# Sharing three pairs of PSUM banks between attention scores and weighting, with a new task order, in a fused attention and gated feed-forward kernel

## The chip, the cores and the metric

The kernel runs on one core of a Trainium2 chip. The metric is the device time of one execution in microseconds (us), the median of three runs. The core has a matrix engine (PE, with the weight loads shown apart as PEld), a vector engine (DVE), an activation engine (ACT), GpSimd (POOL) and a sync engine (SP); the last two issue the transfers here. Matmuls write to PSUM, which the program cuts into eight banks of 512 fp32 columns, numbered 0 to 7.

## The reference, cut to what matters

Attention over 4 batches, 8 heads, 768 positions and head size 64. Heads 0, 2 and 6 are causal over all keys; the other five see a window of 64 keys and 4 sink keys. The heads are then put side by side to a 3072 x 512 matrix `x`, and a gated feed-forward block with a gated residual follows.

```python
stream_keep = causal & (is_sink | in_win)
mask = np.where(retr[0, :, 0, 0, None, None], full_mask, stream_mask)
scores = np.where(mask[None, :, :, :], scores, -1000000000.0)
a = np.exp(scores - np.max(scores, axis=-1, keepdims=True))
a = a / (np.sum(a, axis=-1, keepdims=True) + 1e-09)
attn_out = np.matmul(a, v)
...
g = x @ w_gate                    # 3072 x 512 times 512 x 1536
val = x @ w_val
ffn_out = gelu(g) * val @ w_out   # 1536 x 512
res_gate = 1.0 / (1.0 + np.exp(-(x @ w_res)))
return (x + res_gate * ffn_out).astype(np.float32)
```

## The kernel before

The program is not written as a fixed sequence. It builds a graph of 1,727 tasks (a task is one instruction, or a few on the same engine), and a list scheduler, which runs while the program is built, puts the tasks of every engine in an order. The engines then run these orders as they stand, with semaphores between them. The 3,072 tokens are worked on in six chunks of 512, numbered c = 0 to 5. For each chunk there are score matmuls (`sc`), exponentials on ACT, masks on DVE, weighting with the values (`win`, `av`, `avk`), normalization on DVE, a transpose to features (`xT`), gate and value matmuls (`g`, `v`), gelu on ACT, the product on DVE (`h`), the residual gate (`res`) and the second feed-forward matmul (`ff`). The attention of one chunk is laid between the `res` and `ff` matmuls of the chunk before it.

Three things decide the order. First, the scheduler gives out PSUM banks. A kind of buffer has a cap (how many may be held at once) and a list of the places it may take, tried from left to right:

```python
P_ps = Psum(psum, {
    "av1": (2, one(0, 1)), "av2": (1, [(0, 1)]), "av1": (3, one(0, 1, 6)),
    "sc": (2, [(2, 3), (4, 5)]), "scr": (3, one(5, 4, 3, 2)), "scr0": (3, one(5, 4, 3, 2)),
    "gv": (4, one(6, 7, 5, 4, 3, 2)), "gv0": (4, one(6, 7, 5, 4)), "gvh": (4, one(7, 6, 4, 5)), "out": (2, one(6, 7)), "warm": (1, one(7, 5)),
})
```

(The key "av1" is written twice; the later one holds.) A score unit takes a pair of banks ("sc"), which the exponentials free. One weighting of a pair of heads takes a pair too ("av2"), from its first matmul until the last of its three DVE instructions, the reciprocal and two normalizations, has read it. Chunk 0 is done in halves and its weighting takes single banks ("av1"). Gate and value matmuls use "gv", and `res` and `ff` use "out". Score units of chunks 1 to 5 go in twos; the first of two takes both places before it starts:

```python
sc = ph(c, "sc")[:-1]
for t, u in zip(sc[0::2], sc[1::2]) if c else ():
    t.deps += u.deps
    u.order.append(t)
    for b in u.bufs[:1]:
        t.bufs.append(b)
        ...
```

Second, the kind of array shape that a PE task uses (`mode`): "row" for the scores (64 x 128), "quarter" for the sink scores (64 x 32), "col" for the windows and the first transposes (128 x 64), and none for all that uses the full array. While the PE is in one of the three special shapes, ready tasks of the same shape come first:

```python
away = e == "pe" and mode is not None and t.mode != mode
p_ = t.prio if t.swap is None or not away else t.swap
key = (int(away), p_, t.seq)          # the smallest key is taken
```

Third, the priorities: a rule gives every task one, and a list `HINTS` ("task:priority") overrides 128 of them.

Until the first gate matmul is ready, the PE is kept busy with matmuls of zeros (line 1178, `warm`), whose results nobody reads; the first gate task ends them.

Of the kernel before, what the change touches and what calls it, by code (L numbers as in the profile page):

```python
# [43 lines left out]


HINTS = (
    "0:-96.05 3:-32.5 13:-14.98 398:-205.14 399:-3161.01 400:-242.48 401:-60.67 406:194.11 428:585.68 "
    "430:523.84 442:461.16 444:1172.07 587:-105.78 592:-108.69 613:396.07 617:407.42 620:-11.7 640:556.2 "
    "642:106.88 643:194.09 646:-2979.21 649:-102.44 659:511.02 686:-2.88 687:77.5 695:496.52 696:499.45 "
    "698:-3129.77 703:60.14 704:-184.95 705:-133.38 707:183.02 708:380.49 711:7.46 712:149.85 713:-50.64 "  # L50
    "715:-14.97 722:1121.95 725:480.98 726:449.69 731:-39.24 732:60.67 733:-318.24 737:-43.72 738:419.39 "
    "739:143.85 743:67.93 744:-230.75 746:-318.2 749:428.99 755:137.07 756:5.66 757:60.69 761:-9.34 "
    "762:495.92 764:2489.99 778:1098.32 789:2479.4 791:2501.2 807:953.41 837:1156.8 842:1419.06 877:2567.99 "
    "879:1563.79 880:2429.98 883:2507.13 898:1013.73 933:1964.55 937:1029.47 939:1471.24 940:2476.14 "
    "955:3421 962:3506.26 963:3575.25 971:3584.03 984:2490.73 989:3565.66 1020:3589.17 1022:2520.47 "
    "1036:2494.69 1066:3486.98 1103:3422.44 1109:3530.5 1114:4315.61 1115:4410.02 1124:-926.78 1134:4596.47 "
    "1141:3465.41 1143:2510.98 1146:2495.35 1152:4653.43 1157:112.2 1170:3039.97 1193:107.93 1248:3488.54 "
    "1265:3479.95 1266:4395.47 1271:4430.01 1272:4484.04 1275:-26.92 1284:5420.01 1289:3472.11 1290:4444.38 "
    "1293:-34.14 1295:3453.61 1302:4490.78 1305:3510.02 1316:3998.02 1318:3550.85 1319:3550.87 1320:4107.35 "
    "1349:3529.55 1351:5429.99 1355:3583.42 1414:5485.04 1451:1066.16 1462:4552.31 1474:4473.03 1475:6343.89 "  # L60
    "1480:4497.31 1530:6505.9 1534:2349.36 1556:5501.98 1602:6498.99 1637:6513.87 1670:7448.62 1687:7406.44 "
    "1689:5504.27 "
)

class Task:
# [396 lines left out]
def build_kernel(nc, q, k, v, w_gate, w_val, w_out, w_res, out):  # L462
# [32 lines left out]
    psum = nc.alloc_psum_tensor("ps", [128, 8 * 512], FP32)  # L495
    one = lambda *bs: [(b,) for b in bs]
    P_ps = Psum(psum, {
        "av1": (2, one(0, 1)), "av2": (1, [(0, 1)]), "av1": (3, one(0, 1, 6)),
        "sc": (2, [(2, 3), (4, 5)]), "scr": (3, one(5, 4, 3, 2)), "scr0": (3, one(5, 4, 3, 2)),
        "gv": (4, one(6, 7, 5, 4, 3, 2)), "gv0": (4, one(6, 7, 5, 4)), "gvh": (4, one(7, 6, 4, 5)), "out": (2, one(6, 7)), "warm": (1, one(7, 5)),  # L500
    })

# [726 lines left out]
def bass_duo_attention_split__then__geglu_gated_residual_kernel(  # L1229
    nc: bass.Bass,  # L1230
    q: bass.AP,
    k: bass.AP,
    v: bass.AP,
    is_retrieval: bass.AP,
    n_sink: bass.AP,
    window: bass.AP,
    moe_w_gate: bass.AP,
    moe_w_val: bass.AP,
    moe_w_out: bass.AP,
    moe_w_res: bass.AP,  # L1240
    out: bass.AP,
):
    assert int(n_sink) == N_SINK and int(window) == WINDOW
    build_kernel(nc, q, k, v, moe_w_gate, moe_w_val, moe_w_out, moe_w_res, out)
# [33 lines left out]
```

The softmax here doesn't subtract the row's maximum and nothing guards it: scores larger than these inputs give would overflow.

## Time and profile before

| | |
|---|---|
| time, median of 3 runs | 270.63 us (270.5 to 271.09) |
| span of the profiled execution | 268.8 us |
| PE busy | 264.2 us (98%), 2391 matmuls |
| DVE busy | 140.1 us (52%) |
| ACT busy | 139.9 us (52%) |
| POOL busy | 87.3 us (32%) |
| PE clock granted | 1.000 of full speed, throughout |

A line of the profile's list of groups gives the source line, the engine, the operation, the tiles written and read, the shapes and the count, then the busy time of the group and the mean of one instruction in ns, then the idle time ahead of them and what ended it. Source lines that matter here: 857 scores, 948 sink scores, 981 windows, 991 weighting of causal heads, 1005 weighting of sinks, 1070 transposes to features, 1098 and 1116 gate and value, 1146 `res`, 1161 `ff`, 1178 the matmuls of zeros, 679 the transposes of queries and keys. Matmuls overlap in the pipeline, so the mean of one (379 ns for 512 columns) is its passage and not its share of the engine; the distance between two starts is the share.

### The profile page before, as it was taken

How to read it: one execution, taken by the hardware profiler on the slowest of the kernel's cores; microseconds unless marked ns; L12 is line 12 of the kernel's file. 1: busy time of each engine (PE TensorE's matmuls, PEld its weight loads, DVE VectorE, ACT ScalarE, POOL GpSimd, SP SyncE). 2: the span in 40 equal slices, each digit the busy share in tenths (PEclk: the TensorE clock that was granted, in tenths of full speed). 3: DMA queues.
4: the chain of work that ended last, by engine and by line, in shares of the span. 5: the costliest groups of instructions: out<-in, count | busy, mean ns of one | idle time of the engine just before them, and what ended most of it. 6: DMA issues, size and time to landing. Idle time of an engine off the chain costs nothing.

```text
span 268.8 us, 5676 instructions
## 1 busy us (share of the span) xinstructions
PE 264.2 (98%) x2391; PEld 138.7 (52%) x2391; DVE 140.1 (52%) x273; ACT 139.9 (52%) x215; POOL 87.3 (32%) x124
## 2 busy tenths in 40 slices
PE   8999999999999999999999999999999999999995
PEld 7677465465444455444455444555444455444444
DVE  2698245485264376445476433486145367534344
ACT  3785358783334877136792243984233788233310
POOL 8999508995808029894000000000000000000000
DMA  6999999999999999999994100022000113200013
GB/s 86 171 205 207 185 180 228 169 168 187 171 129 187 154 160 185 216 189 125 184 148 134 41 0 0 2 41 96 25 0 0 39 41 80 78 2 0 1 39 120
DMA packets 97562, 29.38 MB, mean 109 GB/s; under 512 B 85504, under 2 KB 93952, under 8 KB 97536
## 3 DMA queue, kind: packets, MB, share of 16 engines
q0 software_dynamic: 70320, 14.69, 65.5%
q1 hardware_dynamic: 27216, 14.33, 27.9%
q8 instruction: 19, 0.31, 0.5%
q14 instruction: 7, 0.06, 0.1%
HBM read 29.36 MB, written 6.29 MB: 133 GB/s over the span
## 4 chain that ended last, share of the span: by engine, by line
PE 93%; DMA 3%; POOL 1%; DVE 1%; issue 0%; POOLq 0%; DVEq 0%
PE ps L1116 44%; PE ps L1161 23%; PE ps L1146 8%; PE ps L857 5%; PE ps L991 3%; DMA va<-in_v_dram 3%; PE ps L1098 3%; PE ps L981 2%; PE ps L1005 2%; PE ps L1070 1%; POOL qks L555 1%; PE ps L948 1%; PE ps L679 1%; PE ps L1178 1%; DVE otile L1168 0%; DVE otile L1165 0%
## 5 line engine op out<-in xcount | busy, mean ns | idle before, releaser
L1130 DVE SCALAR_TENSOR_TENSOR hT<-gact,ps 128x512 f16<-128x512 f16 x68 | 45.8, 686 | 67.4 <-ACT gact L1128 36.6
L1128 ACT ACTIVATE gact<-ps 128x512 f16<-128x512 f32 x68 | 40.1, 597 | 74.0 <-PE ps L1116 72.5
L1116 PE MATMUL ps<-xT,wv 128*128 128x512 f16 x272 | 74.3, 379 | 0.0
L1116 PE MATMUL ps<-xT,wg 128*128 128x512 f16 x272 | 74.1, 379 | 0.0
L1161 PE MATMUL ps<-wo,hT 128*128 128x512 f16 (+2 forms) x312 | 70.4, 363 | 0.0
L1116 PEld LDWEIGHTS ps<-xT,wg 128*128 128x128 f16 x272 | 26.3, 98 | 31.5 <-ACT xT L1077 0.6
L1116 PEld LDWEIGHTS ps<-xT,wv 128*128 128x128 f16 x272 | 26.2, 98 | 30.5 <-DVE hT L1130 0.5
L1161 PEld LDWEIGHTS ps<-wo,hT 128*128 128x128 f16 x312 | 27.5, 98 | 27.0 <-issue 0.7
L873 ACT ACTIVATE er<-ps 128x1024 f16<-128x1024 f32 (+4 forms) x40 | 34.2, 891 | 9.5 <-PE ps L857 9.4
L555 POOL DMA_DIRECT2D qks<-in_k_dram x36 | 28.3, 827 | 32.4 <-DMA qkt<-qks 21.9
L555 POOL DMA_DIRECT2D qks<-in_q_dram x36 | 28.8, 840 | 0.8 <-POOLq L1260 0.8
L1165 DVE SCALAR_TENSOR_TENSOR otile<-srs,ps 128x512 f32<-128x512 f32 (+2 forms) x26 | 16.8, 644 | 16.5 <-PE ps L1161 16.4
L1146 PE MATMUL ps<-wr,xT 128*128 128x512 f16 x96 | 24.7, 379 | 0.0
L555 POOL DMA_DIRECT2D va<-in_v_dram x24 | 21.6, 926 | 2.7 <-PE ps L1005 2.7
L1149 ACT ACTIVATE srs<-ps 128x512 f32<-128x512 f32 x24 | 14.3, 597 | 15.6 <-PE ps L1146 15.3
L1048 DVE TENSOR_TENSOR xtok<-ps,rcp 128x512 f32<-128x512 f32 (+1 forms) x28 | 16.9, 609 | 0.6
L1168 DVE TENSOR_TENSOR otile<-otile,xtok 128x512 f32<-128x512 f32 (+2 forms) x26 | 16.8, 647 | 0.7
L857 PE MATMUL ps<-qkt 64*128 64x64 f16 (+4 forms) x391 | 16.9, 213 | 0.0
L857 PEld LDWEIGHTS ps<-qkt 64*128 64x128 f16 x391 | 9.8, 94 | 9.4 <-issue 3.4
L873 ACT ACTIVATE es<-ps 128x1024 f16<-128x1024 f32 (+1 forms) x14 | 12.6, 898 | 2.9 <-PE ps L857 2.6
L1146 PEld LDWEIGHTS ps<-wr,xT 128*128 128x128 f16 x96 | 8.7, 98 | 10.0 <-issue 0.7
L1178 PE MATMUL ps<-blank 128*128 128x128 f16 x116 | 11.4, 249 | 1.1 <-DVE blank L527 1.1
(70 smaller groups left out, 212.5 us busy)
## 6 DMA issues: line engine op xcount, KB each, us to landing
out_dram<-otile SPq DMA_DIRECT2D x23, 256.0 KB, 2.2
va<-in_v_dram POOLq DMA_DIRECT2D x24, 128.0 KB, 17.0
qks<-in_k_dram POOLq DMA_DIRECT2D x32, 64.0 KB, 11.9
qks<-in_q_dram POOLq DMA_DIRECT2D x32, 64.0 KB, 12.4
wg<-in_moe_w_gate_dram POOLq DMA_DIRECT2D x3, 512.0 KB, 10.3
wv<-in_moe_w_val_dram POOLq DMA_DIRECT2D x3, 512.0 KB, 10.6
wo<-in_moe_w_out_dram POOLq DMA_DIRECT2D x4, 384.0 KB, 22.2
vs<-va SPq DMA_DIRECT2D x4, 260.0 KB, 7.4
```

The costliest lines, as they stand in the source:

```text
L555: return G.add(eng, issue, lambda e: e.dma_start(out_ap(), in_ap), deps, prio, bufs=bufs, dma=cost, name=name, grp=grp)
L857: return [e.matmul(at(scr)[:, oo:oo + w], lhsT=side(BB, low, 1)[half, k0:k0 + 128], rhs=side(BB, low, 0)[half, qq:qq + w], start=True, sto ...
L873: return e.activation(out=o, in_=i_, func=AF.Exp, scale=SM_SCALE)
L1048: t2 = G.add("dve", c_dve(2 * n * 64), lambda e: e.tensor_tensor(out=xview(), in0=avv(0, DHEAD), in1=scale(), op=ALU.mult), [t1] + xdeps, ...
L1116: return lambda e: [e.matmul(at(dst)[:, :], lhsT=w[:, ci, f * 128:(f + 1) * 128], rhs=at(xtbuf)[:, ci, :], start=(ci == 0), stop=(ci == NC ...
L1128: ta = G.add("act", c_act(512), (lambda gb=gb, ga=ga: lambda e: e.activation(out=at(ga)[:, :], in_=at(gb)[:, :], func=AF.Gelu))(), [tg], p ...
L1130: th = G.add("dve", c_dve(512), (lambda vb=vb, ga=ga, f=f: lambda e: e.scalar_tensor_tensor(out=at(h)[:, f, :], in0=at(ga)[:, :], scalar=0 ...
L1146: e.matmul(at(rb)[:, :], lhsT=at(xtbuf)[:, ci, s], rhs=wr[:, ci, :], start=(ci == 0), stop=(ci == NCB - 1))
L1149: ta = G.add("act", c_act(512), (lambda rb=rb, sr=sr: lambda e: e.activation(out=at(sr)[:, :], in_=at(rb)[:, :], func=AF.Tanh, scale=0.5)) ...
L1161: e.matmul(at(fb)[:, w], lhsT=at(h)[:, fi, s], rhs=wo[:, fi, w], start=(fi == 0), stop=(fi == NF - 1))
L1165: t1 = G.add("dve", c_dve(n), (lambda fb=fb, sr=sr, ot=ot, w=w: lambda e: e.scalar_tensor_tensor(out=at(ot)[:, w], in0=at(sr)[:, w], scala ...
L1168: t2 = G.add("dve", c_dve(n), (lambda ot=ot, lt=lt, w=w: lambda e: e.tensor_tensor(out=at(ot)[:, w], in0=at(ot)[:, w], in1=at(xbuf)[:, lt, ...
```

## The change

The change shares three pairs of banks, (0, 1), (2, 3) and (4, 5), between scores and weighting. A score unit could use two pairs and can now use three, and up to three units may be held at once instead of two. A weighting could use only (0, 1) and now may use any of the three; two weightings may be held at once instead of one. The caps and places of gate, value and output buffers stay as they were. The list of priorities is replaced: 147 entries for 128, and five of the new ones (marked "~") set the priority that a task has while the PE is in another array shape. No task is added or taken away except matmuls of zeros, whose number follows from the schedule; what can change is the order on each engine, the bank that each buffer gets and so the semaphore waits, and, for the few tasks that may run on either DVE or ACT, the engine. The aim is to let scores and weightings run further ahead and stand closer together.

```diff
 HINTS = (
-    "0:-96.05 3:-32.5 13:-14.98 398:-205.14 399:-3161.01 400:-242.48 401:-60.67 406:194.11 428:585.68 "
...
+    "0:-9.51 2:-52.51 4:-44.21 5:-57.18 6:-1060.04 421:-59.16 428:2066.12 430:2989.94 ~430:3531.29 479:1306.02 "
+    "495:1278.68 524:2561.23 596:-96.42 607:1050.19 614:97.41 633:-66.88 636:205.02 640:382.38 ~640:131.36 "
+    "~644:995.57 648:740.75 657:765.41 662:760 664:759.5 666:349.49 668:100.04 691:4.54 696:2962.41 699:1421.49 "
...
+    "956:2754.07 965:4155.32 971:2503.38 972:65.29 993:2397.82 994:2160.7 1002:1679.16 1004:3164.19 "
+    "~1004:3423.66 1009:3163.69 ~1009:2964.44 1029:7296 1037:3619.4 1060:2504.5 1061:4279.31 1064:1096.39 "
...
     P_ps = Psum(psum, {
-        "av1": (2, one(0, 1)), "av2": (1, [(0, 1)]), "av1": (3, one(0, 1, 6)),
-        "sc": (2, [(2, 3), (4, 5)]), "scr": (3, one(5, 4, 3, 2)), "scr0": (3, one(5, 4, 3, 2)),
+        "av1": (3, one(0, 1, 6)), "av2": (2, [(0, 1), (4, 5), (2, 3)]),
+        "sc": (3, [(2, 3), (4, 5), (0, 1)]), "scr": (3, one(5, 4, 3, 2)), "scr0": (3, one(5, 4, 3, 2)),
         "gv": (4, one(6, 7, 5, 4, 3, 2)), "gv0": (4, one(6, 7, 5, 4)), "gvh": (4, one(7, 6, 4, 5)), "out": (2, one(6, 7)), "warm": (1, one(7, 5)),
     })
```

In the new list, entries 0 to 6 are constants built on DVE and POOL, 421 to 430 the first transposes of queries and keys, 596 to 668 the attention of chunk 0 (`sc`, exponentials, masks, normalization), and nearly all of the rest gate, value, `res` and `ff` matmuls of all chunks, with a few score, window and exponential tasks of chunks 2 to 5 among them. The four old entries that placed the copies of the sink values on POOL (398 to 401) are gone, so these copies fall back to their rule.

## The prediction

> **What bounds the kernel now.** I read the first two parts of the page first, because a change of order can only pay where an engine waits.
>
> ```profile
> span 268.8 us, 5676 instructions
> PE 264.2 (98%) x2391; PEld 138.7 (52%) x2391; DVE 140.1 (52%) x273; ACT 139.9 (52%) x215; POOL 87.3 (32%) x124
> PE   8999999999999999999999999999999999999995
> PE 93%; DMA 3%; POOL 1%; DVE 1%; issue 0%; POOLq 0%; DVEq 0%
> ```
>
> The second line is the busy time of each engine, the third the PE in 40 slices, the fourth the chain that ended last, by engine. All three point to the PE: it is busy in every slice and makes up 93% of the chain. But busy is not yet used well: the page counts a matmul's whole passage. So I went to the chain in order of time, where a run of equal matmuls gives the distance between starts.
>
> ```profile
> 107.93 19.86 PE ps L1116 x92
> 231.29 20.72 PE ps L1116 x96
> ```
>
> The columns are start, duration, what, and how many. 19.86/92 and 20.72/96 are both 216 ns for a matmul of 512 columns. This is the pace of the gate and value matmuls for 20 us on end, with not one gap.
>
> The next view is the PE's timeline between 130 and 147 us, one of the stretches in which the attention of a chunk lies between the `res` and `ff` matmuls of the chunk before.
>
> ```profile
> 130.26 1.90 PE L1161 MATMUL ps<-wo,hT 128*128 128x512 f16 x8
> 132.09 0.56 PE L857 MATMUL ps<-qkt 64*128 64x64 f16 x13
> ...
> 138.51 2.32 PE L1161 MATMUL ps<-wo,hT 128*128 128x512 f16 x10
> 140.67 0.77 PE L991 MATMUL ps<-va,er 128*128 128x65 f16 x20
> ```
>
> The columns are start, duration, engine, line, tiles, the part of the array used, shape and count. From 138.51 to 140.67 there are 2.16 us, 10 matmuls at 216 ns: following work of the same full array (128*128) starts at once. From 130.26 to 132.09 there are 1.83 us where 8 x 216 ns are 1.73: the first score matmul (64*128) starts about 0.1 us late. I took the starts of all PE matmuls from the trace and did this for each neighbouring pair: start to start[...]. After 18.65 us, when the last matmuls of zeros are over, there are 89 changes of array shape, and they cost **94.7 ns each in the mean** (half of them between 93.2 and 95.8 ns), 8.43 us together. All other gaps add up to 0.9 us, and most of that looks like records missing from the trace. So from 18.65 us on, the PE waits for no data and no bank that I can find: it pays for work, and for changing shape.
>
> The rest of the span lies at the two ends. Up to 18.65 us, 116 matmuls of zeros take 10.6 us of the PE (sum of their starts to the next start):
>
> ```profile
> L1178 PE MATMUL ps<-blank 128*128 128x128 f16 x116 | 11.4, 249 | 1.1 <-DVE blank L527 1.1
> ```
>
> These are the wait for the first inputs and for chunk 0's attention, in disguise. At the other end the last matmul starts at 265.67 us and 3.1 us follow for the last gated sum and its transfer.
>
> [...] No wait for a bank shows on the PE before; whether one will after, no run shows yet.
>
> **The change, part by part.**
>
> *Matmul work*: none is added or removed. The gate, value, `res` and `ff` matmuls, the scores and the weightings keep their counts and shapes, so the sum of their 216 ns and smaller pieces stays. This is the bulk: 268.8 us, less 10.6 of zeros, 8.4 of shape changes, 0.9 of gaps, 3.1 at the end and 1.1 ahead of the first matmul leaves about 244.7 us that no order can touch.
>
> *A third score unit and a second weighting*: before, a weighting holds banks (0, 1) until the third DVE instruction has read them. A reciprocal is 0.18 us and each of the two normalizations about 0.6 to 0.7 us (609 ns is the mean of the group at line 1048), so some 1.5 us in which no other weighting can start. And two score units wait for both exponentials, 0.9 us each (891 ns at line 873). The PE fills both waits with `res` and `ff` matmuls, at no loss except two shape changes for each visit. With more banks the scheduler may place scores, sink scores and windows of two head pairs next to each other and save visits. That is the only way in which this part can pay after 18.65 us.
>
> How many changes can go? Counted by stretch, before: 10 from 20 to 43.8 us (chunk 0's second half and a few input transposes), then for the attention of chunks 1 to 5: 17, 16, 13, 16 and 16. Chunk 3 shows what the old scheme reaches at its best, because there a sink score is followed at once by scores and scores three times by windows. If the other four come down to chunk 3's 13, that is 4+3+3+3 = 13 changes, 13 x 94.7 ns = **1.23 us**. With a third unit 11 each could be reached, 13 more changes less, 1.2 us again; I don't count on it, since sticking to a shape is already in the scheduler and most of the new priorities are for full-array matmuls. My choice is 1.2 us.
>
> *The start*: 10.6 us of zeros is the greater reserve, but it hangs on input transfers, POOL's issuing (busy 5.00 of 5 us from 5 to 10 and from 15 to 30 us) and ACT. ACT's timeline before 20 us shows exponentials and copies nearly without a break from 8.6 to 19.7 us; its waits for scores there are 0.67, 0.21 and 0.17 us. A third score place can close some of these, at most 1.05 us. The new priorities also bring two mask constants forward and let four copies on POOL (1.54 us at 12.54 us), which stand ahead of three weight transfers, fall behind some of them. I set the start at -0.2 us, with half a microsecond either way.
>
> *The end*: the tail is 3.1 us of DVE and output transfer that the change does not cut; 0.
>
> *New waits*: gate and value matmuls take banks 6, 7, 5, 4, 3, 2. With (2, 3) or (4, 5) held by late weightings, the first gate matmuls of a chunk can run short where they did not before. I add 0.2 us for that.
>
> The sum: 270.6 - 1.2 - 0.2 + 0.2 = **269.4 us**.
>
> **The rivals.** *The order on paper and the chip part ways*: the priorities are fitted to assumed durations, and the engines run the order as it stands. If an exponential, a normalization or a bank comes later than assumed, the PE stands still at that place[...]. Against it: the order before was made in the same way and shows no such stop in 246 us. For it: every bank of the six is now in use by two or three kinds of buffer, and each reuse is a wait across engines. One stop of 0.4 us at each of five attention stretches is 2 us and eats the gain: 271 us. *ACT takes over*: in the stretches from 85 to 90, 95 to 105 and 135 to 140 us, ACT is busy 4.1 to 4.8 of 5 us. A third score unit then only queues ahead of ACT, no exponential ends earlier, and only the shape changes are left: 269.5 to 270.5 us. *The start sets the gain*: if chunk 0's attention really gets closer together, the first gate matmul, at 19.43 us before, moves up by as much as a microsecond, and since the PE is full from there on, all of it reaches the end: 268.2 us. *All is hidden*: the PE is full already, the visits stay as many, and the time stays at 270.6 us.
>
> **Range and chances.** The centre is 269.4 us. The lower end, 267.8, is both halves of the gain at their best: 25 changes less (2.4 us) and 0.5 us at the start. The upper end, 271.0, is no gain in changes and 0.4 us of new waits. Two per cent are 5.4 us: to be that much faster all shape changes but a few would have to go, or half the zeros at the start, for which I see no ground, so 0.03. To be that much slower the PE would have to stop for over 5 us in some new place, so 0.02. Within 2%: 0.95.
>
> **What would show it.** (1) Runs of gate and value matmuls must still go at 216 ns; if not, all of this reading is wrong. (2) The shape changes after the zeros should fall from 89 to about 76, at the same 95 ns. (3) The zeros' share and the start of the first gate matmul (19.43 us) should move by less than 0.7 us. (4) In the list of waits, the PE should still show no wait of note for DVE or ACT; a new entry of the PE waiting for the normalization or for gelu would be the bank shortage. (5) ACT's idle time waiting for scores at line 873, 9.4 us in 18 waits for the causal heads, should fall without the span falling with it. The prediction fails if shape changes do not fall, if PE gaps appear that belong to no shape change, or if the first gate matmul moves by several microseconds.

## The result: slower by 3.2%, and the profile after

| | before | after |
|---|---|---|
| time, median (lowest to highest) | 270.65 us (same chip, beside the changed kernel) | 279.13 us (278.62 to 280.13, 4 runs) |
| ratio, 95% interval | | 1.0319 [1.0296, 1.0343] |
| span of the profiled execution | 268.8 us | 278.3 us (the slowest of the four) |
| shape changes behind the first gate matmul | 88 | 79 |
| matmuls of zeros, their share of the PE | 116, 10.58 us | 112, 10.25 us |
| start of the first gate matmul | 19.43 us | 19.70 us |
| start of the last PE matmul | 265.67 us | 274.43 us |

The 40 slices and the chain of the changed kernel, from its page:

```profile
span 278.3 us, 5663 instructions
...
PE   8999999999997399999999999999999999999994
...
PEclk9999999999999599999999999999999999999999
...
PE 77%; DMA 16%; POOL 2%; DVE 1%; issue 0%; SPq 0%; DVEq 0%
```

A slice is 7.0 us. In slices 13 and 14 the PE falls to 7 and 3 tenths, and in the 14th its clock to 5 tenths; everywhere else the row is as full as before. The chain that ended last has 16% DMA where it had 3%. So the loss is one hole near 90 us and not many small ones. The stretches around it (columns: window, its length, busy time and count of PE, PEld, DVE, ACT and POOL, clock, DMA engines busy, GB/s):

```profile
85.00:90.00 5.00, 3.75 (x40) 1.60 (x38) 2.46 (x5) 4.13 (x6) 2.81 (x4) 1.00 2.03 166
90.00:95.00 5.00, 0.00 (x0) 0.00 (x0) 0.81 (x2) 0.00 (x0) 0.00 (x0) 0.68 1.59 160
95.00:100.00 5.00, 4.76 (x43) 2.25 (x44) 0.69 (x1) 2.45 (x4) 0.00 (x0) 0.64 1.47 117
```

From 90 to 95 us not one matmul starts. The PE's timeline names what ended the hole, in brackets (idle time, releaser):

```profile
85.99 2.76 PE L1163 MATMUL ps<-wo,hT 128*128 128x512 f16 x12
95.24 0.61 PE L859 MATMUL ps<-qkt 64*128 64x512 f16 x1 [6.49 <-DMA q<-qkt]
...
96.21 3.06 PE L1148 MATMUL ps<-wr,xT 128*128 128x512 f16 x8
99.20 0.61 PE L859 MATMUL ps<-qkt 64*128 64x64 f16 x13
```

(Line numbers are 2 higher than before.) Two things are to be seen. The PE stood for 6.49 us for a transfer, `q<-qkt`, and for no bank. And behind the hole 8 `res` matmuls take 2.99 us from 96.21 to 99.20, where 8 x 216 ns are 1.73: 1.2 us more, at the clock of 0.64 in the window above. With the score matmuls ahead of them, which are slow too, it is 1.6 us.

`q<-qkt` is a copy that SyncE starts: it puts the transposed queries and keys of head 6 for one chunk on the other 64 partitions, where a part of this head's scores is computed. What it waited for stands in the chain in order of time (start, duration, what):

```profile
64.85 21.52 DMA va<-in_v_dram
86.39 0.46 SPq L640
...
87.15 8.05 DMA q<-qkt
...
95.24 1.03 PE ps L859 x16
```

The load of values `va` took 21.52 us from issue to landing. Then SyncE (SPq) issued line 640, and 0.76 us after it the copy `q<-qkt`. Line 640 is `vs<-va`, a copy of these values for the windows, which the PE needs much later. The copy `q<-qkt` does not need the values at all; it only stands behind two copies `vs<-va` in SyncE's order. SyncE's timeline after:

```profile
85.20 1.64 SPq L640 DMA_DIRECT2D vs<-va  x2
87.15 0.66 SPq L732 DMA_DIRECT2D q<-qkt  x1
```

and before:

```profile
80.81 0.67 SPq L730 DMA_DIRECT2D q<-qkt  x1
...
92.76 1.81 SPq L638 DMA_DIRECT2D vs<-va  x3
```

The order of these copies has turned round. The values come no later than before (landed at 86.37 us, before at 87.50). But the copy `q<-qkt` goes out 6.34 us later and lands at 95.20 us instead of 87.58, while the PE is ready for its scores at about 88.7 us. Before, it started them at 88.81 us without a wait:

```profile
87.85 1.03 PE L1161 MATMUL ps<-wo,hT 128*128 128x512 f16 x4
88.81 0.61 PE L857 MATMUL ps<-qkt 64*128 64x64 f16 x13
```

How the order turned can be followed in the scheduler's plan of the two kernels, that is, the times that it gives to all tasks while it makes the order. It assumes that the values for these two copies are there at 72.5 and 74.0 us (on the chip 85.12 and 86.37) and the features for `q<-qkt` at 78.6 us. The plan of the kernel before has them nearly as early (74.5 and 75.4 us), but there transposes of a better priority (1050 against 1051; the smaller goes first) fill SyncE until `q<-qkt` is ready. The new list moves two of these transposes, tasks 479 and 495, back to 1306 and 1279. SyncE then runs out of other work and takes the two copies first. In the plan each of the two entries is needed for this: without either one `q<-qkt` goes first again. They are not enough by themselves: with the same list and the old table of banks the plan has the values at 78 and 79 us, and `q<-qkt` goes first.

### The profile page after: what moved, and what is told of

It is laid out like the page before. It is cut to its first block, busy times and chain, and to the rows that moved or that the text cites. A ratio compares the mean times of both kernels' runs of the same rounds, so it can differ in the third digit from the quotient of the medians.

```text
span 278.3 us, 5663 instructions
## 1 busy us (share of the span) xinstructions
PE 265.9 (96%) x2387; PEld 140.7 (51%) x2387; DVE 140.5 (51%) x272; ACT 138.2 (50%) x216; POOL 87.2 (31%) x124
## 4 chain that ended last, share of the span: by engine, by line
PE 77%; DMA 16%; POOL 2%; DVE 1%; issue 0%; SPq 0%; DVEq 0%
PE ps L1118 35%; PE ps L1163 21%; DMA va<-in_v_dram 8%; PE ps L1148 8%; DMA wv<-in_moe_w_val_dram 5%; PE ps L859 4%; DMA q<-qkt 3%; PE ps L993 3%; PE ps L983 2%; PE ps L1007 1%; PE ps L1100 1%; POOL va L557 1%; PE ps L681 1%; PE ps L1072 1%; PE ps L950 1%; POOL wg L557 1%
## 5 line engine op out<-in xcount | busy, mean ns | idle before, releaser
L1118 PE MATMUL ps<-xT,wv 128*128 128x512 f16 x272 | 72.0, 380 | 0.4 <-DMA wv<-in_moe_w_val_dram 0.4
L1118 PE MATMUL ps<-xT,wg 128*128 128x512 f16 x272 | 71.6, 380 | 0.0
L1163 PE MATMUL ps<-wo,hT 128*128 128x512 f16 (+2 forms) x312 | 69.4, 363 | 0.0
L1148 PE MATMUL ps<-wr,xT 128*128 128x512 f16 x96 | 25.7, 394 | 0.0
L1180 PE MATMUL ps<-blank 128*128 128x128 f16 x112 | 12.1, 262 | 1.1 <-DVE blank L529 1.1
```

The source lines that it names most:

```text
L1118: return lambda e: [e.matmul(at(dst)[:, :], lhsT=w[:, ci, f * 128:(f + 1) * 128], rhs=at(xtbuf)[:, ci, :], start=(ci == 0), stop=(ci == NC ...
L1148: e.matmul(at(rb)[:, :], lhsT=at(xtbuf)[:, ci, s], rhs=wr[:, ci, :], start=(ci == 0), stop=(ci == NCB - 1))
L1163: e.matmul(at(fb)[:, w], lhsT=at(h)[:, fi, s], rhs=wo[:, fi, w], start=(fi == 0), stop=(fi == NF - 1))
```

## The experiments

**Theory A**: the time is lost because `q<-qkt` of chunk 2 stands behind two transfers in SyncE's order that wait for a slow load. The main rivals: the shared banks and the new order of the PE cost it, in many waits; or the new order of transfers on POOL does, by delaying the loads. For the first runs a helper was put behind the scheduler that takes tasks out of one engine's order and puts them ahead of another task; the dependences and the waits are then worked out for that order.

### One copy ahead of two, nothing else

```diff
     span = G.schedule()
+    move("sp", (476,), 491)          # q<-qkt of chunk 2 ahead of the two vs<-va
```

> The changed kernel with one transfer moved in SyncE's order: the copy of half of the features of batch 1 (q<-qkt, 87.15 us in the changed kernel's trace) is issued ahead of the two copies vs<-va of batch 2 (85.20 and 86.39 us) and not behind them. All other engines keep their order. Theory A (the two copies wait for values of batch 2 that land at 86.37 us, and hold up the copy behind them): the copy goes out at about 82.4 us, lands near 89.5 us, the PE waits about 1 us where it waited 6.5 us, the slow clock of the PE after the wait (1.2 us) goes, and the time is 272 to 273 us. Theory B (the banks or the new order of scores make the PE stop there anyway): the wait stays above 5 us and the time above 277 us.

Measured: 271.78 us median of 13 runs (270.59 to 272.67 us, and one of 275.13 us), ratio to the kernel before 1.0035 [1.0018, 1.0051]. The copy was issued at 80.84 us and landed at 87.78. From the PE's timeline:

```profile
87.82 0.39 PE L859 MATMUL ps<-qkt 64*128 64x512 f16 x1 [0.53 <-DMA q<-qkt]
...
88.38 1.90 PE L1148 MATMUL ps<-wr,xT 128*128 128x512 f16 x8
```

The stop has shrunk from 6.49 to 0.53 us, and 8 `res` matmuls are back at 216 ns each (88.38 to 90.21 us, with 0.1 us for the change of shape behind them). One place in one queue, with all banks and all priorities as changed, carries all of the 3.2% but 0.35. The PE runs the same 2,387 matmuls in the same order in both kernels, so their starts can be set against each other. The changed kernel's lag grows by 1.5 us at two value weights, by 6.0 us at the stop and by 1.6 us in the slow matmuls behind it, 9.0 us in all between these two executions. The last two make 7.5 us; the medians differ by 7.35. The value weights are taken up below.

### The mirror: two copies ahead of one in the kernel before

```diff
     span = G.schedule()
+    move("sp", (491, 492), 476)      # the two vs<-va ahead of q<-qkt
```

> The kernel before with the reverse edit: the two copies vs<-va of batch 2 are put ahead of the copy q<-qkt of batch 1 in SyncE's order; banks and priorities as before. Theory A: the values of batch 2 land at 87.50 us in the trace before, so the copy goes out near 89 us instead of 80.81 and lands near 96.5 us; the PE, which needs it at 88.9 us, stops for about 7 us and runs about 3 us at a lower clock after it: 278 to 280 us. Theory B (the banks or the new order of scores are the cause): below 272 us.

Measured: 279.25 us, 4 runs, ratio 1.0321 [1.0306, 1.0337]. From SyncE's and then the PE's timeline:

```profile
83.61 2.63 SPq L638 DMA_DIRECT2D vs<-va  x2
86.54 0.66 SPq L730 DMA_DIRECT2D q<-qkt  x1
```

```profile
94.94 0.61 PE L857 MATMUL ps<-qkt 64*128 64x64 f16 x12 [5.83 <-DMA q<-qkt]
...
95.91 1.89 PE L1161 MATMUL ps<-wo,hT 128*128 128x512 f16 x4
```

With the old banks and the old priorities the same turn of the order makes the whole loss: the same stop, and behind it 4 matmuls in 1.68 us (95.91 to 97.59), 420 ns each. Removal and addition agree, so A is shown as the cause of the loss; how much of the rest the banks and priorities carry is the next question.

### POOL's order as before, beside the first cure

```diff
+    move("sp", (476,), 491)
+    G.prog["pool"][:27] = [... the order of the kernel before ...]
```

> The changed kernel with the copy q<-qkt first, and besides the first 27 POOL instructions (constants, first loads, copies of sink values) in the order of the kernel before. Theory C (the new POOL order lets the first two parts of the value weights land 1.5 and 2.3 us later than before, and the PE waits 0.87 and 0.57 us for them): the two waits go and the time is about 1.4 us under that of the copy first alone, 270.5 to 271.5 us. Rival D (the weights are later [...], whatever the order on POOL): the same time as with the copy first alone, within 0.4 us.

Measured: 271.7 us, 5 runs, ratio 1.0037 [1.0023, 1.0051], the same as without it. POOL's order is not what is left. In the changed kernel's profile the PE had stood idle 0.7 and 0.4 us for value weights (0.87 and 0.57 us when counted between the starts of matmuls); with POOL's order as changed, the first experiment had these weights 1.5 and 2.4 us earlier, so those waits are most likely a spread of the transfers between executions.

### Each half of the change alone

The table of banks alone, with the old priorities:

```diff
-        ... "av2": (1, [(0, 1)]), "av1": (3, one(0, 1, 6)),
-        "sc": (2, [(2, 3), (4, 5)]), ...
+        "av1": (3, one(0, 1, 6)), "av2": (2, [(0, 1), (4, 5), (2, 3)]),
+        "sc": (3, [(2, 3), (4, 5), (0, 1)]), ...
```

> The kernel before with only the table of banks changed: three pairs shared, up to three score units and two weightings; the old priorities. In the order that the scheduler then gives, SyncE issues the copy q<-qkt of batch 1 ahead of the copies vs<-va, so theory A expects no stop of 6 us there. The order has 145 matmuls of zeros instead of 116, so the first gate matmul comes some 1.5 us or more later. Expected 273 to 282 us; if the banks by themselves were a gain, it would lie under 270 us.

The new priorities alone, with the old table (the same two lines, the other way round, in the changed kernel):

> The changed kernel with the old table of banks (two score units, one weighting): only the new priorities are left. In the order that the scheduler then gives, SyncE issues the copy q<-qkt ahead of the copies vs<-va, so theory A expects no stop of 6 us at that place. The priorities were chosen for the other table; the PE changes array shape 129 times instead of 118. Expected: slower than the kernel before by waits at other places, 276 to 288 us; if the priorities by themselves were a gain, under 270 us.

Measured: 278.54 us for the table alone (1.0293 [1.0272, 1.0313]), 290.24 us for the priorities alone (1.0725 [1.07, 1.0751], above the 276 to 288 us expected), 2 runs each. From the list of waits, table alone and then priorities alone (columns: total us, times, longest):

```profile
PE ps L857 <- ACT er L873: 1.9, 2, 1.3
...
PE ps L1070 <- DVE x L1046: 0.9, 1, 0.9
```

```profile
PE ps L983 <- DVE xtok L1050: 3.4, 2, 1.7
...
PE ps L1072 <- DVE x L1048: 2.7, 3, 1.1
...
PE ps L1118 <- DVE xT L1079: 2.2, 4, 0.9
```

In the first, SyncE's order is the good one, and yet the PE stops, for exponentials and normalizations. In the second the windows (line 983) wait for the normalization `xtok` of the weighting before, because there is one place for weightings and the priorities assume two; the transposes (line 1072) and gate and value matmuls (line 1118) then wait for their own late inputs. These two numbers do not add up to the 3.2%: a list of priorities is fitted to one table, and with another it gives another order in all engines. So the halves can't be read as the shares of the change. They show only that the table does not pay without a list of its own. Most of these losses are in the plan already: there the halves take 274.6 and 281.1 us, against 265.5 for the kernel before and 264.7 for the changed one.

### Ahead of the late copy, other work

In the first experiment the PE still waited 0.53 us. Here four `res` matmuls stand ahead of these scores:

```diff
+    move("sp", (476,), 491)
+    move("pe", (971,), 999)          # one res group ahead of the score pair
```

> The changed kernel with the copy q<-qkt first, and on the PE one group of four res matmuls (0.86 us) put ahead of the pair of score units that needs the copy. With the copy first alone the time was 271.78 us in the middle but 270.6 us at its best, and the PE reaches the pair at 87.0 us where the copy lands at 87.8. If that short wait is what is left of the loss (theory A, second half), the time falls by 0.3 to 1 us, to 270.7 to 271.5 us, and scatters less; if the rest comes from elsewhere, it stays at 271.5 to 272.

Measured: 271.46 us, 22 runs, ratio 1.0029 [1.0014, 1.0044]. The wait is gone from the PE's timeline, there is no bracket any more:

```profile
88.54 1.03 PE L1148 MATMUL ps<-wr,xT 128*128 128x512 f16 x4
89.50 0.39 PE L859 MATMUL ps<-qkt 64*128 64x512 f16 x1
```

The median moved by 0.3 us, within the intervals, and the times do not scatter less, as was expected: nine lie from 270.17 to 270.94 us, eight from 272.27 to 272.76 and five between. So the wait of 0.5 us is not what is left. The profiled execution is one of the eight; its first gate matmul starts at 21.09 us, against 19.70 in the profile of the first experiment. ACT's timelines, of the first experiment and then of this one:

```profile
16.86 0.60 ACT L875 ACTIVATE es<-ps 128x512 f16<-128x512 f32 x1 [0.60 <-PE ps L983]
```

```profile
18.26 0.60 ACT L875 ACTIVATE es<-ps 128x512 f16<-128x512 f32 x1 [1.24 <-PE ps L983]
```

Chunk 0's exponentials run 1.4 us later in this execution, where a load of queries had landed at 9.85 us instead of 8.39. The profiled execution with POOL's order as before is of the same kind: first gate matmul at 21.07 us, 272.07 us in all. The likely reading is that the new start hands a late load on to the end, and the old one, whose 27 runs beside these lie between 270.3 and 271.7 us, less so. No run changed the start alone, so this stays open.

### The scheduler told of late loads

In the plan by which the changed order was made, the last of the values that the two copies need is there at 74.0 us. On the chip it landed at 86.37. Here the plan is given later landings, and the list of priorities is searched anew, once with the new table and once with the old:

```diff
+    BB.vtok[i].late = (1.3, 1.3, 10.0, 7.0)[b]             # values of batch b, us
...
+    t.late = 4.0                                          # q<-qkt
+    d.late = (5.0, 5.0, 5.0, 11.0, 8.5, 8.5)[c]            # queries and keys of chunk c
-    HINTS = ...                                           # old list
+    HINTS = ...                                           # list found with these numbers
```

> The new table of banks, with the scheduler told of later landings (values of batch 2 by 8.7 us and of batch 3 by 5.7, queries and keys of chunks 3 to 5 by 6 and 3.5 us, the copies vs<-va by 3 and q<-qkt by 2), as the trace of the kernel before shows them, and the priorities searched anew under these. In its order the copy q<-qkt goes out ahead of the copies vs<-va. Theory A (what was wrong was the assumed landing, not the table): no PE stop near 88 us, 269.5 to 271.5 us. If the shared banks make stops of their own: above 272 us.

> The old table of banks with the same later landings and priorities searched anew in the same way for as long: what the refit does without the shared banks. If the table is worth something, this is slower than the refit with the new table by over 0.5 us; if the table is worth nothing, the two lie within 0.5 us of each other, 269.5 to 271 us.

Measured, on one chip: 272.88 us with the new table (1.0068 [1.0044, 1.0091]), 272.42 us with the old (1.0055 [1.0042, 1.0068]), 6 runs each. The largest wait for data in each:

```profile
PE ps L959 <- DMA q<-qkt: 1.6, 1, 1.6
```

```profile
PE ps L793 <- DMA qks<-in_q_dram: 1.4, 2, 0.8
```

The large hole is gone in both, but both are slower than expected and neither beats the kernel before. The new table's 272.88 us lies where stops by the shared banks were expected (above 272 us); its list of waits names none, its largest wait is for `q<-qkt` again. Under equal treatment the intervals of the two tables overlap: no gain of the shared banks was found. The search was a short one, so this is no proof that there is none.

### One priority taken out

```diff
-    "... 430:2989.94 ~430:3531.29 479:1306.02 "
+    "... 430:2989.94 ~430:3531.29 "
```

> The changed kernel with one of its 147 priorities taken out (that of task 479, a transpose of chunk 3's features that SyncE starts); bank table and all other priorities as changed. The scheduler then has two more of these transposes ahead on SyncE and puts the copy q<-qkt of chunk 2 ahead of the two copies vs<-va by itself, without a hand in the order. From there on the rest of the order differs too. Theory A (a transfer that waits for the values of batch 2 holds up the queue behind it): the copy is issued by 85 us, the PE does not stop for more than 2 us near 88 us, no half clock there, and the time falls to 271 to 275 us; it need not reach the kernel before, because the other priorities were fitted to an order that no longer holds. Rival (the shared banks and the new order of the PE cost the time at many places): the time stays above 277 us.

Measured: 284.65 us, 4 runs, ratio 1.0526 [1.0504, 1.0547]. The expectation failed, and the time lies where the rival had it (above 277 us). `vs<-va` did fall behind `q<-qkt`, and yet the copy was issued at 88.43 us. From the chain in order of time:

```profile
64.69 22.23 DMA qks<-in_q_dram
...
86.94 1.19 SPq L724
...
88.43 6.51 DMA q<-qkt
...
94.98 1.03 PE ps L859 x17
```

The queue was now held by a transpose (line 724) whose queries, of the next chunk, took 22.23 us to land. I had put a name to the blocking transfer and not looked at what else would stand ahead. Of the rest of the 14 us some 4 lie near 117 us: the PE waits 1.93 us for a normalization and 0.61 us for the transposed input, and its clock is 0.84 and 0.82 in the two windows of 5 us from 115 us on, up to 1.7 us more. The plan already has this order as a worse one: 271.1 us without the entry, 264.7 with it.

To see whether this is the same cause with another holder, the copy was put ahead of that one transpose:

```diff
+    move("sp", (476,), 504)          # q<-qkt ahead of the transpose that waits
```

> The kernel of the last run, in which the copy q<-qkt stood behind a transpose that waited for queries of chunk 3 (landed 86.92 us) and was issued at 88.43 us, with this one copy put ahead of that one transpose in SyncE's order; nothing else differs. Theory A (what the PE pays is the place of the copy behind any transfer that waits for a late load): the copy is issued near 81 us, lands by 88.5 us, the stop of 6.4 us near 88.6 us and the half clock behind it (about 1.2 us) are gone, and the time falls from 284.65 by 7 to 8 us, to 276.7 to 277.7 us; the stop of 1.9 us for the normalization near 117 us stays. Rival (a PE that is held up once by late loads is held up a little later by the next one, so that the gain is given back): less than 4 us is gained.

Measured: 276.95 us, 4 runs, ratio 1.0219 [1.0159, 1.0278], 7.7 us less than without it. The copy was issued at 81.76 us and landed at 88.73, the scores started at 88.78 us with no wait on the PE, and the wait for the normalization stayed, as expected. A holds for both holders that were tried: a transfer that waited for a late load held up the ready copy behind it. Of the 6 us that remain against the kernel before, the plan of this order has 5.6 (271.1 against 265.5).

## Why the prediction was wrong, point by point

The prediction was 269.4 us, 267.8 to 271.0; 279.13 us was measured. The differences in the profiled executions, taken from the starts of all matmuls (the changed kernel's is its slowest, so they add up to more than the 8.5 us between the medians):

| term | predicted | measured |
|---|---|---|
| shape changes | -1.2 us (13 fewer) | -0.85 us (9 fewer) |
| start (first gate matmul) | -0.2 us | +0.27 us |
| new waits | +0.2 us | +6.56 us at `q<-qkt`, +1.44 us for value weights |
| PE clock | not considered | +1.57 us |
| other gaps | not considered | -0.2 us |
| last PE start, sum | -1.2 us | +8.76 us (274.43 - 265.67) |
| tail behind it | 0 | +0.8 us |

*The step that failed* is "New waits", with its 0.2 us. It looked for waits at the banks of gate and value matmuls, and none is there. The waits came from SyncE's queue, which the prediction never opened: it put down "the PE waits for no data and no bank" for the order before and went on as if a new order would keep that. The profile of before already held what was needed. The PE started the scores at 88.81 us and their copy had landed at 87.58, a margin of 1.2 us. A load of values needed 21 us from issue to landing and came at 87.50. And the list of priorities has three entries (479, 495 and 524) that are SyncE's transposes; I had read the list as one of PE tasks with a few others.

What the prediction had not looked at shows in the traces. SyncE waited in its queue for the load and issued the copy `q<-qkt` only 0.76 us after the `vs<-va` that had waited; with the same list and only these copies put the other way round (the first experiment) the copy went out at 80.84 us. And the PE was slower behind the stop: after 6.5 us of stop the traces have 3.4 us at up to 427 ns a matmul, about twice 216; in the mirror the slow part behind the stop lasted 5.1 us. The last two experiments have it too, with stops of 1.93 and 0.61 us close together: shortly behind them two value matmuls take 0.85 us, 425 ns each, and the granted clock (0.84 and 0.82 in two windows of 5 us, then 0.66 in one of 5 us) makes it about 3.4 us at half the clock, an estimate from these windows.

*Work and pace* (check 1) held: away from the hole the gate and value matmuls kept their 216 ns. *Shape changes* (check 2): the cost of one was right, 93 to 96 ns for the middle half, counted as the distance between two starts less the pace of that many columns (in runs of one full-array shape 216 ns for 512 columns, 109 for 256, 56 for 128 and 29 for 65, the median in both profiles); the count was mis-sized, 9 fewer and not 13. Four of the nine went in the second half of chunk 0, which the prediction had not counted on; the attention of chunks 1 to 5 has 17, 15, 12, 14 and 15. *Zeros and start* (check 3): the first gate matmul moved by 0.27 us, below the 0.7 allowed, but in the wrong direction. *Bank shortage* (check 4): the changed kernel shows no wait of the PE for the normalization or gelu; with the same priorities and one place for weightings the windows waited 3.4 us for it, and in the changed kernel 10 of 20 weightings and 19 of 61 score units stand in a pair of banks that they could not take before. *ACT's wait for causal scores* (check 5) fell from 9.4 us in 18 to 4.2 us in 7, and no shorter span came of it, as the prediction said.

*Of the rivals*, "the order on paper and the chip part ways" was right in kind: values of batch 2 come 12 us later than the plan had them. It was wrong in place, five stops of 0.4 us at the attention against one of 6.5 us, and in size, and "no such stop in 246 us" was weak evidence, since it spoke for one order and its luck. "ACT takes over" and "the start sets the gain" did not happen. "All is hidden" comes closest once the copy is put right: 1.0035 and 1.0029, a little above the kernel before. The chance of 0.02 for a slowdown of over 2% rested on "the PE would have to stop for over 5 us in some new place", which is just what it did.

## What to carry to other kernels

When a change touches a schedule, read the order of the queues that start transfers as closely as that of the engines that compute: for every transfer on them, what it waits for, what stands behind it, and by how much the next reader misses it. A copy that waits for a load of unsure time belongs behind all the copies whose data are there; here this order alone gave back 7.35 us. An order that is fitted to assumed durations is only as good as its smallest margin on the chip (1.2 us at this copy, against a load that came 12 us later than planned), so list those margins before the new order is trusted.

## What the runs showed of the hardware

The stop of 6 us on the PE cost more than itself: 1.6 us of slow matmuls behind it in the changed kernel, and 2.4 us in the mirror (each against the same matmuls at full speed). The clock was 0.50 for 6.83 us both times (the changed kernel, then the mirror; columns as in the windows above):

```profile
91.77:98.60 6.83, 3.36 (x24) 1.68 (x25) 0.69 (x1) 1.49 (x2) 0.00 (x0) 0.50 1.51 137
```

```profile
93.20:100.03 6.83, 5.09 (x25) 1.91 (x25) 0.76 (x2) 2.42 (x3) 0.00 (x0) 0.50 1.66 154
```

Only the part behind the stop cost time, and how long that was differed: the PE started again at 95.24 us in the first and at 94.94 us in the second.

The loads of values (128 KB each) that POOL started between 62 and 72 us took 17 to 22 us from issue to landing in the profiles before and after. SyncE's copies `vs<-va` and `q<-qkt` issued between 80 and 95 us took 6.8 to 8.1 us. `q<-qkt` took 6.78 us before and 8.05 after, so issued 6.34 us later it landed 7.62 us later.
